# Block sums of v for the second batch by VectorE halving additions, second queries in two other banks, and placements issued ahead of loads

## The chip, the cores and the metric

The kernel runs on one core of one Trainium2 chip. The metric is the device time of one execution in microseconds (us). The engines are TensorE (PE; its weight loads are listed as PEld), VectorE (DVE), ScalarE (ACT), GpSimd (POOL) and the queue of SyncE (SP, listed as SPq), which issues every DMA of this kernel. Each works through its own list in order and waits on semaphores.

## The reference

Three stages follow each other: a sparse attention, a feed-forward layer with h * cos(h), and a second one with a normalised product. The change touches the attention and the first feed-forward steps behind it.

```
B, H, S, D = 2, 8, 768, 64;  block, window = 32, 16
k_sum = k.reshape(B, H, 24, 32, D).max(axis=3)
v_sum = v.reshape(B, H, 24, 32, D).mean(axis=3)
scores_l = q @ k.T / 8, kept where abs(i - j) < 16
scores_s = q @ k_sum.T / 8 + log(32)
a = softmax(concat(scores_l, scores_s))
out = a @ concat(v, v_sum)
x = out as [1536, 512]
h = x @ w_in;  x = (h * cos(h)) @ w_out
h = x @ w_in2; ln = normalised(h * softmax(h)) * g_ln;  out = ln @ w_out2
```

## The kernel before, in words

**Attention.** The 16 heads are worked in 8 pairs (n = 0 to 7; pairs 0 to 3 are the first batch, 4 to 7 the second), and each pair in 3 groups of four tiles of 64 queries, so there are 24 groups G. One loop, `for step in range(NGR + LA)`, runs 29 steps (0 to 28) as a software pipeline written by hand: step s issues the scores of group s+1 (`emit_s`, PE, tile `sps`), the masked maximum of group s (`emit_max`, DVE, then a subtraction by POOL), the exponential of s-1 (ACT), the sum and reciprocal of s-2 (DVE) with the normalising product (POOL), the transposes of s-4 (`emit_t`, PE, tile `aps`) with their copy out (`emit_at`), and the product with v of s-5 (`emit_av`, PE, tile `ops`) with its copy out (`emit_x`). Order within an engine is the order in which the code issues. The scores have two PSUM banks, used in turn, so the scores of G+2 can begin only when the maximum of G has read its bank.

**Keys and queries of a pair.** In the middle group of a pair (g == 1) `pair_k` and `pair_q` copy the loaded heads side by side (DVE for later pairs). In the last group (g == 2) PE transposes them (`emit_k`, `emit_q`) into the one tile `qk`; ACT then copies the queries out (`emit_qx`), DVE takes block maxima (`emit_ksum`), and ACT lays out the windows (`emit_kx`, `emit_kx_ends`). For pair 0 the queries go to two banks of their own, and DVE copies them out.

**v.** `load_v` fetches per pair 96-row windows with four DMAs into one of four buffers `vt`. Rows 96 to 119 of `vt` hold the 24 block means. `sum_v` makes the sums on PE with 12 matmuls against a strip of ones (tile `vsum`; the trace counts 24), `scale_v` scales them on ACT (`vm`), and `place_vsum` writes them with two DMAs. `VSUM_AT` gives the step of each pair; placement is issued at the end of the next step, behind that step's loads.

**Weights and fill.** The first feed-forward weights are turned into two parts beside the attention: ACT rewrites the raw words, DVE joins them (L171), ACT and POOL split them (L186, L187). `FILL` puts 3 or 4 of the first h products on PE per step from step 15. `drain` runs the cosine part of the first h tiles: u (ACT), n (DVE), sin (ACT), r (DVE), g (ACT and DVE). In the last steps DVE copies out the transposes (`DVE_AT` = 20) and the attention's result. Then the dense part begins with `emit_y(0)`.

## Time and profile before

| what | value |
|---|---|
| time, median of 3 runs | 496.52 us (492.27 to 496.61) |
| profiled execution: time, span | 493.17 us, 491.4 us |
| busy in the span: PE, DVE, ACT, POOL | 479.3, 303.0, 313.6, 152.6 us |
| 0 to 31.04 us (start, up to the scores of step 6): PE, DVE, ACT, POOL busy | 24.96, 17.46, 13.76, 13.11 us |
| 31.04 to 85.23 us (steps 6 to 21) | 53.96, 43.91, 45.67, 46.16 us of 54.19 |
| 85.23 to 103.49 us (steps 22 to 28) | 15.71, 15.70, 12.62, 10.33 us of 18.26 |
| 103.49 to 491.40 us (dense part) | 384.71, 225.98, 241.56, 82.97 us of 387.91 |

The span is what the trace covers; 1.77 us of the time lie around it. A row of the chain of waits has a start, a length and the work that the end hung on. A row of the timeline has a start, a length, the engine, the line and what it wrote from what; in brackets stands how long the engine stood idle before it and what ended that. "PEclk" is the granted TensorE clock as a share of 2.4 GHz.

### The profile page before, as it was taken

How to read it: one execution, taken by the hardware profiler on the slowest of the kernel's cores; microseconds unless marked ns; L12 is line 12 of the kernel's file. 1: busy time of each engine (PE TensorE's matmuls, PEld its weight loads, DVE VectorE, ACT ScalarE, POOL GpSimd, SP SyncE). 2: the span in 40 equal slices, each digit the busy share in tenths (PEclk: the TensorE clock that was granted, in tenths of full speed). 3: DMA queues.
4: the chain of work that ended last, by engine and by line, in shares of the span. 5: the costliest groups of instructions: out<-in, count | busy, mean ns of one | idle time of the engine just before them, and what ended most of it. 6: DMA issues, size and time to landing. Idle time of an engine off the chain costs nothing.

```text
span 491.4 us, 7884 instructions
## 1 busy us (share of the span) xinstructions
PE 479.3 (98%) x2943; PEld 394.5 (80%) x2943; DVE 303.0 (62%) x666; ACT 313.6 (64%) x539; POOL 152.6 (31%) x146
## 2 busy tenths in 40 slices
PE   8789999899999999999999999999999999999997
PEld 5668887678888888888888888888888888888886
DVE  3668976883445446556474655556477776776661
ACT  3669878756685766556655653788624867777621
POOL 3469977722432222222222220245500011110000
PEclk9889999999999999999999999999999999999999
DMA  8987854201222322332223220220001333223211
GB/s 258 285 199 210 212 135 127 87 2 43 87 85 90 122 88 87 92 122 88 87 91 120 88 86 27 94 96 0 0 2 43 87 90 83 65 64 65 69 40 43
DMA packets 59046, 46.17 MB, mean 94 GB/s; under 512 B 40448, under 2 KB 51328, under 8 KB 59008
## 3 DMA queue, kind: packets, MB, share of 16 engines
q1 hardware_dynamic: 59008, 45.67, 32.4%
q8 instruction: 23, 0.38, 0.3%
q14 instruction: 15, 0.12, 0.1%
HBM read 36.61 MB, written 3.15 MB: 81 GB/s over the span
## 4 chain that ended last, share of the span: by engine, by line
PE 88%; SPq 5%; POOL 2%; DVE 1%; ACT 1%; issue 1%; DMA 1%
PE y L276 27%; PE h L234 25%; PE o L865 13%; PE h L751 13%; PE sps L510 3%; SPq L393 3%; PE ops L565 2%; PE aps L547 2%; PE vsum L421 2%; SPq L357 1%; SPq L389 1%; POOL sm L525 1%; PE tp L799 1%; DMA vt<-vm 1%; POOL sm L540 1%
## 5 line engine op out<-in xcount | busy, mean ns | idle before, releaser
L234 PE MATMUL h<-xs,w 128*128 128x512 f32 x576 | 141.2, 391 | 0.0
L276 PE MATMUL y<-gs,w 128*128 128x512 f32 x576 | 138.1, 389 | 0.0
L276 PEld LDWEIGHTS y<-gs,w 128*128 128x128 f32 x576 | 108.1, 188 | 22.4
L234 PEld LDWEIGHTS h<-xs,w 128*128 128x128 f32 x576 | 107.2, 188 | 21.6
L187 POOL TENSOR_TENSOR w<-s,w 128x512 fp32r<-128x512 f32 x48 | 62.2, 1295 | 164.9 <-ACT w L186 141.9
L243 ACT ACTIVATE r<-h 128x512 int32<-128x512 f32 x48 | 28.7, 597 | 85.9 <-PE h L234 85.9
L248 DVE SCALAR_TENSOR_TENSOR r<-r,h 128x512 f32<-128x512 int32 x48 | 33.0, 687 | 67.4 <-ACT r L243 67.3
L865 PE MATMUL o<-w,ls 128*128 128x512 f32 (+1 forms) x312 | 67.8, 373 | 0.0
L751 PE MATMUL h<-w,xs 128*128 128x512 f32 x288 | 67.6, 390 | 0.0
L171 DVE SCALAR_TENSOR_TENSOR s<-raw 128x512 int32<-128x512 int32 x48 | 37.9, 790 | 44.8 <-ACT raw L164 38.3
L865 PEld LDWEIGHTS o<-w,ls 128*128 128x128 f32 x312 | 55.3, 188 | 10.7 <-DVE ls L841 0.4
L751 PEld LDWEIGHTS h<-w,xs 128*128 128x128 f32 x288 | 53.9, 188 | 11.1
L786 POOL TENSOR_TENSOR st<-st,mhalf 128x1 f32<-128x1 f32 x12 | 6.6, 550 | 110.1 <-DVE st L785 101.7
L204 POOL TENSOR_TENSOR xs<-X,xs 128x512 fp32r<-128x512 f32 x22 | 29.6, 1353 | 32.7 <-ACT xs L203 32.7
L253 ACT ACTIVATE r<-r,half_pi 128x512 f32<-128x512 f32 x48 | 34.5, 718 | 1.3 <-DVE r L248 1.3
L264 DVE TENSOR_TENSOR gs<-h,gs 128x512 fp32r<-128x512 f32 x48 | 32.6, 680 | 4.2 <-ACT gs L263 4.0
L258 DVE TENSOR_TENSOR h<-h,r 128x512 f32<-128x512 f32 x48 | 32.9, 686 | 0.4 <-ACT r L253 0.4
L163 ACT ACTIVATE raw<-raw 128x512 f32<-128x512 f32 x48 | 31.9, 664 | 0.0
L164 ACT ACTIVATE raw<-raw 128x512 int32<-128x512 uint32 x48 | 31.8, 663 | 0.0
L186 ACT ACTIVATE w<-s 128x512 fp32r<-128x512 f32 x48 | 30.1, 626 | 1.2 <-DVE s L171 0.9
L768 ACT ACTIVATE e<-h,st 128x1024 f32<-128x1024 f32 (+1 forms) x13 | 13.6, 1049 | 26.6 <-DVE st L764 23.1
L525 POOL TENSOR_TENSOR sm<-sm,mx 128x480 f32<-128x480 f32 x24 | 26.1, 1090 | 9.8 <-DVE mx L521 9.5
(81 smaller groups left out, 570.3 us busy)
## 6 DMA issues: line engine op xcount, KB each, us to landing
raw<-in_moe_w_in_dram SPq DMA_DIRECT2D x24, 512.0 KB, 3.6
raw<-in_moe_w_out_dram SPq DMA_DIRECT2D x24, 512.0 KB, 3.3
vt<-in_v_dram SPq DMA_DIRECT2D x16, 240.0 KB, 3.5
kt<-in_k_dram SPq DMA_DIRECT2D x8, 384.0 KB
qt<-in_q_dram SPq DMA_DIRECT2D x8, 384.0 KB, 7.7
out_dram<-osb SPq DMA_DIRECT2D x11, 256.0 KB, 2.0
vt<-vm SPq DMA_DIRECT2D x16, 72.0 KB
vt<-in_v_dram SPq DMA_DIRECT2D x16, 48.0 KB, 4.1
```

Source lines behind the costliest of these rows:

```text
L163: nc.scalar.activation(out=hw, in_=hw, func=AF.Prelu, scale=REBIAS, alpha=NEGATIVE)
L164: nc.scalar.activation(out=lw, in_=lw.bitcast(U32), func=AF.Copy, scale=TOP3)
L171: nc.vector.scalar_tensor_tensor(out=self.f32[i], in0=t[:, :, 1], scalar=3, in1=t[:, :, 0], op0=ALU.logical_shift_left, op1=ALU.bitwise_or)
L187: nc.gpsimd.tensor_tensor(out=w[:, 1, :], in0=f, in1=as32(w[:, 0, :]), op=ALU.subtract)
L234: nc.tensor.matmul(h, lhsT=w[:, a, f * P:(f + 1) * P], rhs=xs_of[tb, c][:, b_, :], start=(m == 0), stop=(m == 3 * KC - 1))
L248: nc.vector.scalar_tensor_tensor(out=r, in0=r.bitcast(I32), scalar=TWO_PI, in1=h_of[step], op0=ALU.mult, op1=ALU.subtract)
L253: nc.scalar.activation(out=r, in_=r, func=AF.Sin, scale=-1.0, bias=half_pi)
L258: nc.vector.tensor_tensor(out=h, in0=h, in1=r, op=ALU.mult)
L264: nc.vector.tensor_tensor(out=gs[:, 1, :], in0=r, in1=as32(gs[:, 0, :]), op=ALU.subtract)
L276: nc.tensor.matmul(y[e], lhsT=w[:, a, e * P:(e + 1) * P], rhs=gs[:, b_, :], start=(f == 0 and i == 0), stop=(f == GF - 1 and i == 2))
L751: nc.tensor.matmul(banks[n], lhsT=xs_of[NTB + t // TPB, c][:, a, t0:t0 + P], rhs=weights.done[w2i[c][n]][:, b_, :], start=(m == 0), stop=( ...
L865: nc.tensor.matmul(o, lhsT=ls_of[t][f // 4][:, a, s0:s0 + P], rhs=w[:, b_, cols], start=(f == 0 and i == 0), stop=(f == NF2 - 1 and i == 2))
```

## The change

It has five parts. (1) For the second batch, `load_blocks` loads v again for four heads at a time with each block of 32 rows on one of 96 partitions; `sum_blocks` adds halves on DVE (1024, 512, 256, 128 and 64 elements per partition), and `place_blocks` scales on ACT and writes with four DMAs. PE's sums for pairs 4 to 7 go. (2) The queries of pair 1 use the two banks of pair 0's, and DVE copies them out, after the keys' windows have been issued. (3) v of pair 0 is loaded before keys and queries of pair 2, its sums move from step 3 to step 1, and all placements move to the head of the next step, ahead of that step's loads. (4) The cosine steps of the first h tiles follow a table: u and n of tiles 0 and 1 come in steps 22 and 23. (5) All transposes are copied out by ACT, and that copy is issued before the drain.

```diff
@@ -94,7 +94,6 @@
     WSTEPS = (4, 7, 10, 13, 16, 19, 20, 21)
     XS = (7, 10, 13, 16)
     IDLE = (0, 0, 0)
-    DVE_AT = 20
     DVE_X = 19
     DVE_NORM = 99
     LAST = 5
@@ -321,15 +320,22 @@
 
         nc.scalar.activation(out=small[:, 1:2], in_=small[:, 0:1], func=func)
 
-    STAGES = ((emit_sin, 2), (emit_r, 2), (emit_u, 1), (emit_n, 1), (emit_g, 2))
+    DRAIN = {
+        -2: ((emit_u, 0), (emit_n, 0)),
+        -1: ((emit_u, 1), (emit_n, 1)),
+        1: ((emit_sin, 0), (emit_r, 0)),
+        2: ((emit_sin, 1), (emit_r, 1), (emit_g, 0), (emit_u, 2), (emit_n, 2)),
+        3: ((emit_sin, 2), (emit_r, 2), (emit_g, 1)),
+        4: ((emit_g, 2),),
+        5: ((emit_u, 3), (emit_n, 3), (emit_sin, 3), (emit_r, 3)),
+    }
 
     def drain(k):
 
         if k == 0:
             table(AF.Sin)
-        for stage, at in STAGES:
-            if 0 <= k - at < GF and (stage, k - at) != (emit_g, GF - 1):
-                stage(k - at)
+        for stage, step in DRAIN.get(k, ()):
+            stage(step)
 
 
     def attention():
@@ -413,9 +419,7 @@
 
             def sum_v(n):
 
-                o = (ps_h0 if n < 6 else ps_qk).tile(
-                    [P, 512] if n < 6 else [P, 2, 2, S // 2], F32, tag="h" if n < 6 else "qk", name="vsum")
-                o = (o if n < 6 else o[:, 0, 0])[:, 0:P]
+                o = ps_h0.tile([P, 512], F32, tag="h", name="vsum")[:, 0:P]
                 for t in range(HALF):
                     for c in range(2):
                         nc.tensor.matmul(
@@ -423,6 +427,35 @@
                             rhs=v_t[n][0:WIN, HALF * c + t].rearrange("p j d -> p (j d)"),
                             start=(t == 0), stop=(t == HALF - 1))
                 vs_t[n] = o
+
+            vb_t, vb_sum = {}, {}
+            HEADS = 4
+
+            def load_blocks(i):
+
+                b, h = divmod(HEADS * i + NPAIR, H)
+                t = vb_t[i] = io.tile([HEADS * NS, BLOCK, D], F32, tag="vb", name="vb", bufs=1)
+                nc.sync.dma_start(
+                    out=t.rearrange("p k d -> p (k d)"),
+                    in_=v[b, h:h + HEADS].rearrange("h (b k) d -> (h b) (k d)", k=BLOCK))
+
+            def sum_blocks(i, half):
+                if not half:
+                    vb_sum[i] = io.tile([HEADS * NS, D], F32, tag="vbs", name="vbs", bufs=1)
+                t = vb_t[i]
+                for m in ((16,), (8, 4, 2, 1))[half]:
+                    nc.vector.tensor_tensor(
+                        out=t[:, 0:m] if m > 1 else vb_sum[i].rearrange("p (k d) -> p k d", k=1),
+                        in0=t[:, 0:m], in1=t[:, m:2 * m], op=ALU.add)
+
+            def place_blocks(i):
+                m = io.tile([HEADS * NS, D], F32, tag="vbm", name="vbm", bufs=1)
+                nc.scalar.activation(out=m, in_=vb_sum.pop(i), func=AF.Copy, scale=1.0 / BLOCK)
+                for h in range(HEADS):
+                    n, j = divmod(HEADS * i + NPAIR + h, 2)
+                    nc.sync.dma_start(
+                        out=v_t[n][WIN:KW, :, j, :],
+                        in_=m[h * NS:(h + 1) * NS].unsqueeze(1).to_broadcast([NS, NT, D]))
 
             def scale_v(n):
                 m = io.tile([P, 2 * D], F32, tag="vm", name="vm")
@@ -475,7 +508,7 @@
                     out=kx[:, :, WIN:KW], in_=ks_t.pop(n).unsqueeze(1).to_broadcast([P, NT, NS]), func=AF.Copy)
 
             def emit_q(n):
-                if n == 0:
+                if n < 2:
                     qk_t["q", n] = bank(2, "q0"), bank(3, "q1")
                 t, (a, b) = q_t.pop(n), qk_t["q", n]
                 for c in range(NR):
@@ -487,7 +520,7 @@
                 qx = io.tile([P, S], F32, tag="qx", name="qx")
                 rows = qx.rearrange("p (i r) -> p i r", r=NR)
                 src = qk_t.pop(("q", n))
-                if n == 0:
+                if n < 2:
                     for r in range(2):
                         nc.vector.tensor_scalar_mul(
                             rows[:, :, r * NR // 2:(r + 1) * NR // 2],
@@ -549,10 +582,7 @@
 
             def emit_at(G):
                 at = sm_p.tile([KW, NG, P], F32, tag="at", name="at", bufs=2)
-                if G >= DVE_AT:
-                    nc.vector.tensor_copy(at, at_t[G])
-                else:
-                    nc.scalar.activation(out=at, in_=at_t[G], func=AF.Copy)
+                nc.scalar.activation(out=at, in_=at_t[G], func=AF.Copy)
                 at_t[G] = at
 
             def emit_av(G):
@@ -586,9 +616,9 @@
             nc.sync.dma_start(out=mask.rearrange("p t k -> p (t k)"), in_=c_mask)
             load_k(1)
             load_q(1)
+            load_v(0)
             load_k(2)
             load_q(2)
-            load_v(0)
             nc.gpsimd.memset(small, 0.0)
             nc.gpsimd.memset(strip, 0.0)
             warm_up(8)
@@ -607,7 +637,9 @@
 
 
             LX, LN, LT, LA = 1, 2, 4, 5
-            VSUM_AT = {3: 0, 4: 1, 7: 2, 9: 3, 12: 4, 13: 5, 16: 6, 19: 7}
+            VSUM_AT = {1: 0, 4: 1, 7: 2, 9: 3}
+            VB_LOAD = {9: 0, 15: 1}
+            VB_SUM = {12: (0, 0), 14: (0, 1), 17: (1, 0), 19: (1, 1)}
             VLOAD_AT = {1: 1, 4: 2, 6: 3, 8: 4, 10: 5, 13: 6, 16: 7}
             for step in range(NGR + LA):
                 n, g = divmod(step, GPP)
@@ -615,6 +647,8 @@
                 ahead = 1 if step == 1 else n + 1 if g == 0 and 0 < n < NPAIR - 1 else 0
 
                 warm_up(IDLE[g] if step < min(FILL) else 0)
+                if step - 1 in VSUM_AT:
+                    place_vsum(VSUM_AT[step - 1])
                 if step + 1 < NGR:
                     emit_s(step + 1)
                 if step == 0:
@@ -648,9 +682,9 @@
                     emit_max(step)
                 if step == 1:
                     emit_ksum(ahead)
-                drain(step - NGR)
                 if LT <= step < NGR + LT:
                     emit_at(step - LT)
+                drain(step - NGR)
                 weights.finish()
                 if summed:
                     emit_norm(step - LN)
@@ -660,7 +694,6 @@
                     emit_kx(ahead)
                 if step == 1:
                     emit_kx_ends(1)
-                if step == 0:
                     emit_qx(1)
                 if g == 2 and n + 2 < NPAIR:
                     emit_qx(n + 2)
@@ -680,8 +713,12 @@
                     load_q(n + 3)
                 if step in VLOAD_AT:
                     load_v(VLOAD_AT[step])
-                if step - 1 in VSUM_AT:
-                    place_vsum(VSUM_AT[step - 1])
+                if step in VB_LOAD:
+                    load_blocks(VB_LOAD[step])
+                if step in VB_SUM:
+                    sum_blocks(*VB_SUM[step])
+                    if VB_SUM[step][1]:
+                        place_blocks(VB_SUM[step][0])
                 if step in VSUM_AT:
                     scale_v(VSUM_AT[step])
 
@@ -889,8 +926,7 @@
 
         for c in range(KC):
             xs_of[1, c] = split_x(1, c, xs_b, nc.vector if c % 2 else nc.gpsimd)
-        for k in range(LAST, 7):
-            drain(k)
+        drain(LAST)
         emit_y(0)
         emit_y(1)
         for step in range(4, NSTEP):
```

**SP in the first steps.** Of before, from the loads of q of pair 3 on (`kt`, `qt`, `vt` are the loads of k, q, v; `vt<-vm` is a placement):

```order
L357 DMA qt<-in_q_dram 128x2x384
L389 DMA vt<-in_v_dram 96x10x64
L393 DMA vt<-in_v_dram 96x2x64
L389 DMA vt<-in_v_dram 96x10x64
L393 DMA vt<-in_v_dram 96x2x64
L139 DMA raw<-in_moe_w_in_dram 128x1024 x2
L357 DMA kt<-in_k_dram 128x6x128
L357 DMA qt<-in_q_dram 128x2x384
L389 DMA vt<-in_v_dram 96x10x64
L393 DMA vt<-in_v_dram 96x2x64
L389 DMA vt<-in_v_dram 96x10x64
L393 DMA vt<-in_v_dram 96x2x64
```

Right behind these stand the four placements of pairs 0 and 1. Of the change, from the same load on:

```order
L363 DMA qt<-in_q_dram 128x2x384
L395 DMA vt<-in_v_dram 96x10x64
L399 DMA vt<-in_v_dram 96x2x64
L395 DMA vt<-in_v_dram 96x10x64
L399 DMA vt<-in_v_dram 96x2x64
L469 DMA vt<-vm 12x12x128 x2
L138 DMA raw<-in_moe_w_in_dram 128x1024 x2
L363 DMA kt<-in_k_dram 128x6x128
```

The placement of pair 0 now stands in front of two weight loads and of the loads of pair 4's k and q and of pair 2's v.

**DVE at steps 14 and 15.** Of the change, from the end of the maximum of step 14 (`mx`) to the first instruction of the maximum of step 15 (`vb` is the tile of blocks, `vbs` the sums, `ss` the softmax sums):

```order
L554 ISA mx 128x1
L170 SCALAR_TENSOR_TENSOR s<-raw 128x512
L447 TENSOR_TENSOR vb<-vb 96x512
L447 TENSOR_TENSOR vb<-vb 96x256
L447 TENSOR_TENSOR vb<-vb 96x128
L447 TENSOR_TENSOR vbs<-vb 96x64
L567 TENSOR_REDUCE ss<-sm_98 128x4
L568 RECIPROCAL ss<-ss 128x4
L488 TENSOR_REDUCE ksum<-qk 128x24
L554 ISA sm_100,mx<-sps,mask 128x120
```

Before, the reduction of `ss` followed the joining of the weight (`s<-raw`) directly. The addition of 1024 stands two steps earlier, behind the maximum of step 12.

**ACT in the last steps.** Of the change, from the copy of step 24's transposes (`at`) on (`r<-h` is u, `r<-r,half_pi` the sine, `gs` g):

```order
L585 ACTIVATE at<-aps 120x512
L321 ACT_TABLE_LOAD
L321 ACTIVATE small<-small 128x1
L585 ACTIVATE at<-aps 120x512
L252 ACTIVATE r<-r,half_pi 128x512
L585 ACTIVATE at<-aps 120x512
L252 ACTIVATE r<-r,half_pi 128x512
L262 ACTIVATE gs<-h 128x512
L242 ACTIVATE r<-h 128x512
L585 ACTIVATE at<-aps 120x512
```

Before, ACT had no copy of transposes there, four u and three sines and g stood behind the table load, and DVE made the copies.

## Rows read from the trace of the kernel before

**Rows 1.** The chain that ended last, shares of the span by engine (page)

```profile
PE 88%; SPq 5%; POOL 2%; DVE 1%; ACT 1%; issue 1%; DMA 1%
```

**Rows 2.** The same chain in order of time: start us, us, what

```profile
26.10 1.00 SPq L436
27.15 2.90 DMA vt<-vm
...
39.58 0.66 PE qk L443 x6
...
57.59 0.97 PE sps L510 x16
...
61.49 0.71 ACT qx L496
...
64.05 1.04 PE sps L510 x16
...
66.98 1.31 PE vsum L421 x24
...
77.69 1.41 PE vsum L421 x24
```

**Rows 3.** Timeline of the first steps: start us, us, engine, line, out<-in

```profile
12.18 0.81 ACT L496 ACTIVATE qx<-qk 128x768 f32<-128x768 f32 x1 [1.76 <-PE qk L482]
13.03 0.96 DVE L455 TENSOR_REDUCE ksum<-qk 128x24 f32<-128x768 f32 x1 [1.40 <-ACT qx L496]
14.41 3.36 SPq L393 DMA_DIRECT2D vt<-in_v_dram  x1
15.66 1.04 PE L510 MATMUL sps<-kx,qx 64*64 64x120 f32 x16 [2.54 <-ACT kx L474]
...
22.13 1.04 PE L510 MATMUL sps<-kx,qx 64*64 64x120 f32 x16
...
25.14 1.04 PE L510 MATMUL sps<-kx,qx 64*64 64x120 f32 x16
...
30.19 0.92 PE L565 MATMUL ops<-at,vt 120*64 120x64 f32 x16 [2.12 <-DMA vt<-vm]
...
34.48 1.04 PE L510 MATMUL sps<-kx,qx 64*64 64x120 f32 x16
```

**Rows 4.** Windows of PE: length, busy (instructions), granted clock, DMA share, GB/s

```profile
17.00:18.00 1.00, 1.00 (x6) 0.50 0.56 123
...
19.00:20.00 1.00, 1.00 (x10) 0.50 0.81 225
31.00:32.00 1.00, 1.00 (x12) 0.50 1.11 231
```

**Rows 5.** DVE additions by line: ns minimum/median/maximum, first and last start, forms

```profile
L204 DVE TENSOR_TENSOR xs<-X,xs x2: 1321/1550/1778, 105.3 to 106.5; 128x512 fp32r<-128x512 f32 x2
L841 DVE TENSOR_TENSOR ls<-s,ls x18: 677/684/1800, 382.2 to 467.2; 128x512 fp32r<-128x512 f32 x18
L771 DVE TENSOR_TENSOR e<-h,e x13: 692/1224/1225, 356.2 to 473.3; 128x1024 f32<-128x1024 f32 x11, 128x512 f32<-128x512 f32 x2
L787 DVE TENSOR_TENSOR st<-st x12: 159/160/161, 360.5 to 477.5; 128x1 f32<-128x1 f32 x12
```

**Rows 6.** Timeline: the two POOL instructions beside DVE's two of line 204

```profile
104.72 3.00 POOL L204 TENSOR_TENSOR xs<-X,xs 128x512 fp32r<-128x512 f32 x2 [8.74 <-ACT xs L203]
```

**Rows 7.** Windows: length, busy of PE, PEld, DVE, ACT, POOL, clock, DMA

```profile
50.63:64.05 13.42, 13.30 (x209) 11.19 (x208) 12.12 (x47) 11.41 (x25) 12.49 (x11) 1.00 0.77 186
64.05:68.29 4.24, 4.24 (x65) 3.50 (x67) 4.21 (x13) 3.67 (x8) 4.17 (x5) 1.00 0.37 129
68.29:85.23 16.94, 16.82 (x231) 13.61 (x230) 10.59 (x54) 13.46 (x28) 12.87 (x13) 1.00 0.58 144
```

**Rows 8.** Waits of PE from 84 to 104 us: total us, times, longest

```profile
PE aps L547 <- DVE at L553: 1.6, 2, 0.9
PE aps L547 <- ACT at L555: 0.8, 2, 0.5
```

## What I predict

> **What bounds the kernel now.** The chain of waits comes first: PE holds 88% of it [rows 1], and from 103.49 us on PE is busy 384.71 of 387.91 us, in work that the change leaves alone. So the change can act only on the moment at which the dense part begins. The chain in order of time then says what that moment hangs on: in the first 30 us on SP and a placement of v [rows 2], later on PE with the sums of v on it (1.31 and 1.41 us) [rows 2]. The timeline of the start shows three PE waits or slow stretches that belong together: scores of step 2 wait 2.54 us, behind block maxima that themselves waited 1.40 us for ACT's copy of the queries [rows 3]; the first product with v waits 2.12 us for its placement [rows 3]; and after each of the two idle stretches the granted clock is 0.50, so 1.2 instead of 2.4 GHz, for about 3 us [rows 4]. Last, the windows of the middle show who could become the bound when PE sheds work: in 50.63 to 64.05 us DVE is busy 12.12 of 13.42 us and POOL 12.49 [rows 7]. DVE and POOL are nearly as full as PE there.
>
> **The start: queries of pair 1, v first, placements ahead.** The block maxima no longer stand behind ACT's copy, so they start at 13.03 - 1.40 = 11.63 us. From their start to the scores it took 15.66 - 13.03 = 2.63 us [rows 3], so these could start at 14.26. The sums of pair 0, 1.31 us [rows 2], now fill PE's idle time, which began at 15.66 - 2.54 = 13.12, and end at 14.43; I take that, 1.2 us earlier than before. DVE's two query copies replace its 1.40 us of idle time. Then come scores (0.97), transposes of keys (0.66) and of queries (the same again) [rows 2]: 16.72. From the start of a query copy to the scores that wait for it it takes 64.05 - 61.49 = 2.56 us [rows 2], so the scores of step 4 start at 19.28 instead of 22.13 [rows 3]. From there to the next scores 25.14 - 22.13 = 3.01 us [rows 3], so 22.29; and from those to the scores two steps on 64.05 - 57.59 = 6.46 us, in a stretch with the same work and no wait for a placement [rows 2]: 28.75 instead of 34.48 [rows 3]. That is 5.7 us. The placement of pair 0 is not what comes late next: its sums end at 14.43, SP is free at 14.41 + 3.36 = 17.77 [rows 3], and four placements took from 26.10 to 30.05 [rows 2], so two land before 21.8. PE asks for them 30.19 - 2.12 - 25.14 = 2.93 us after the scores at 22.29 [rows 3], at 25.2; 3.4 us are the cover. What does come late is PE itself: with the sums moved away from step 3 it idles from 16.72 + 0.97 = 17.69 to 19.28, 1.6 us. Idle stretches of 2.54 and 2.12 us were each followed by the half clock [rows 3, 4]; three us at 0.50 lose 1.5. So the gain is 5.7 without and 4.2 with such a stretch. The nearest row, 2.12 us, speaks for it; I take **-4.5 us**. Keys and queries of pair 2 now load behind 576 KB of v; DVE, their first user, has the two query copies to do before them, and that is the cover. If it is too short, each us that they land late is lost at the scores of step 4.
>
> **The first load of blocks, steps 12 to 15.** PE sheds two sums, 2.6 us. DVE gets five additions. An addition of 1024 takes 1.224 us, of 512 0.684, of one element 0.160 [rows 5]; on the line between the last two, 256, 128 and 64 take 0.42, 0.29 and 0.23. Each waits for the one before it, so they add up: 1.22 + 0.68 + 0.42 + 0.29 + 0.23 = 2.84 us. They also meet POOL. DVE's additions with both inputs in SBUF took 0.684 alone and 1.321 and 1.778 beside POOL [rows 5], while POOL's two took 3.00 us [rows 6]: a wait of 0.64 and 1.09 us each. POOL is busy 93% of the stretch [rows 7], so each of five additions can wait between 0 and 1.09; half of that, 0.5, is 2.5 us. DVE's demand is then 12.12 + 2.84 + 2.5 = 17.46 us in a stretch of 13.42, or **+4.0 us**. The ends are 12.12 + 2.84 - 13.42 = +1.5 (no wait at all) and, with five times 1.09, +7.0. Nothing of PE's 2.6 us comes through, since the next scores wait for DVE's maximum, and that stands behind the additions. ACT's scaling of the sums waits for the last addition at the head of ACT's queue, with the split of a weight, an exponential and a copy of transposes behind it; POOL and PE wait for these. This is inside the +7.0. The extra load of 768 KB meets DMA shares of 0.77, 0.37 and 0.58 [rows 7], and its placements are wanted three steps later, in step 17: nothing.
>
> The Trainium skill (SBUF — State Buffer, Who interferes with whom) says that a VectorE instruction with two SBUF inputs and a GpSimd instruction that reads SBUF shut each other out, the later one waiting until the other is finished. It speaks against this change, since by it a short addition waits as long as a long one. A reader of the rows alone might take a factor, 1.55 / 0.684 = 2.27, and get 2.84 x 2.27 = 6.4 us of additions and +5.1 us for this stretch instead of +4.0.
>
> **The second load, steps 16 to 21.** PE sheds 1.31 + 1.41 = 2.7 us [rows 2]. DVE is busy 4.21 + 10.59 of 21.18 us [rows 7], so 6.4 us are idle and the additions, 2.84 + 2.5 = 5.3, have room on the whole. But one addition stands ahead of the block maxima and four ahead of a maximum for which scores wait, so I take **0**, with -2.7 (all hidden) and 5.3 - 2.7 = +2.6 (nothing hidden) as ends.
>
> **The last steps.** PE waited 1.6 us for DVE's copies of transposes and 0.8 for ACT's [rows 8]. ACT now issues these copies ahead of the cosine work, and four of the first tiles' instructions move into steps 22 and 23. I take **-1.6 us**; the ends are -2.4 and 0, the latter if the n of tiles 0 and 1, which now stand ahead of the last weights on DVE, hand their delay on through POOL.
>
> **Sum.** -4.5 + 4.0 + 0 - 1.6 = -2.1 us, and 493.17 - 2.1 = 491.1, so 491 us. The profiled execution was 3.35 us below the median of the runs shown and 0.9 above the lowest. About 1%, 4.9 us, is what a measurement of this kernel can tell from no change.
>
> **Rivals.** (a) *The additions are hidden.* POOL waits for DVE's results, so it may run dry whenever DVE is late, and the additions meet nobody. For it: POOL's next operands come from DVE's maximum and reciprocal. Against it: POOL busy 93%. Then +1.5 in the first stretch and -2.7 in the second: -4.5 + 1.5 - 2.7 - 1.6 = -7.3, so 485.9 us. (b) *The start does not move.* The change then doesn't do what it says: v of pair 0, or the keys and queries behind it, land too late, and only the 1.2 us of the first scores come: -1.2 + 4.0 - 1.6 = +1.2, so 494.4 us. For it: the DMA queue had SP held for 3.36 us at one load [rows 3]. Against it: the same bytes in another order. (c) *Slower: DVE's additions take the place of PE as the bound in both stretches.* Each addition waits a full POOL instruction, 1.09 us, which decides from about 0.9 on; PE then idles over 4 us at step 15 and gets the half clock once more, 1.5 us: -4.2 + 7.0 + 2.6 + 1.5 = +6.9, so 500.1 us. For it: the two rows beside POOL [rows 5]. Against it: POOL has few instructions ready while DVE stands still.
>
> **How the numbers follow.** Forecast 0.46, with 488 to 494 as its own range; (a) 0.32, 483.5 to 488; (b) 0.12; (c) 0.10. Faster by over 1% means below 488.2: 0.9 of (a) and about an eighth of the forecast, 0.34. Slower by over 1% means above 498.1: most of (c), 0.08. The rest is 0.58. The range from 485 to 497.5 leaves out a third of (a) and most of (c), under 2 in 10.
>
> **What will show it.** Start: the scores of step 2 near 14.4 us, no wait of the first product with v for a placement, the scores of step 7 between 28.8 and 30.3; the clock at 0.50 or not near 21 us tells the two ends apart. First load: additions of 1024 longer than 1.3 us and of 64 near 0.23 plus a wait, and PE waiting for DVE's maximum at step 16; additions at their bare prices speak for (a). Last steps: no PE wait for copies of transposes. I am wrong if PE stays full through steps 12 to 16, or if the start to step 7 moves by less than 3 us.

## The result: 0.5% slower, and what the profile after shows

The kernel after took 496.07 us, the median of 20 runs (493.71 to 498.32); the kernel before, beside it, 493.62 of 20 (490.99 to 496.61). The ratio is 1.0052, with a 95% interval of 1.0034 to 1.0069, so 1.7 to 3.4 us slower. I had forecast 2.1 us faster. The profiled execution of after took 494.23 us with a span of 492.4, against 493.17 and 491.4 before: 1.06 us. It lies 1.84 us below its median, that of before 0.45 below its own, which is the rest of the difference.

Chain of waits of after, shares by engine, the line that answers to [rows 1]:

```profile
PE 83%; DVE 8%; ACT 3%; DMA 2%; SPq 2%; issue 1%; POOL 0%; DVEq 0%; ACTq 0%
```

DVE holds 8% where it held 1%. **The start** moved by nearly what I had said. Timeline of PE's first steps in after, as in [rows 3] (start us, us, engine, line, out<-in, idle time before):

```profile
14.95 1.04 PE L543 MATMUL sps<-kx,qx 64*64 64x120 f32 x16
...
17.86 1.04 PE L543 MATMUL sps<-kx,qx 64*64 64x120 f32 x16 [0.42 <-DVE mx L554]
20.29 1.04 PE L543 MATMUL sps<-kx,qx 64*64 64x120 f32 x16 [1.39 <-DVE mx L554]
...
26.17 0.69 PE L595 MATMUL ops<-at,vt 120*64 120x64 f32 x16
...
29.84 1.04 PE L543 MATMUL sps<-kx,qx 64*64 64x120 f32 x16 [0.82 <-DVE mx L554]
```

Scores of step 2 start at 14.95 instead of 15.66, the first product with v waits for no placement, and scores of step 7 start at 29.84 instead of 34.48: 4.64 us. What came late were keys and queries of pair 2; DVE's copies of them stand ahead of the maxima for which the scores of steps 3 and 4 wait:

```profile
14.27 0.56 DVE L381 COPY kg<-kt 128x768 f32<-128x768 f32 x1 [0.95 <-DMA kt<-in_k_dram]
...
15.59 0.56 DVE L381 COPY qg<-qt 128x768 f32<-128x768 f32 x1 [0.77 <-DMA qt<-in_q_dram]
```

**The first load of blocks** then takes a part back. Timeline of DVE, POOL and ACT around its additions (DVE L447):

```profile
48.82 1.45 DVE L447 TENSOR_TENSOR vb<-vb 96x1024 f32<-96x1024 f32 x1
49.16 1.97 POOL L558 TENSOR_TENSOR sm<-sm,mx 128x480 f32<-128x480 f32 x1
...
55.79 1.44 POOL L558 TENSOR_TENSOR sm<-sm,mx 128x480 f32<-128x480 f32 x1
56.30 2.92 DVE L447 TENSOR_TENSOR vb<-vb 96x512 f32<-96x512 f32 x3
57.19 1.43 POOL L573 TENSOR_TENSOR sm<-sm,ss 128x480 f32<-128x480 f32 x1
59.26 0.22 DVE L447 TENSOR_TENSOR vbs<-vb 96x64 f32<-96x64 f32 x1
59.52 0.26 ACT L453 ACTIVATE vbm<-vbs 96x64 f32<-96x64 f32 x1 [2.48 <-DVE vbs L447]
```

Five additions take 1.45 + 2.92 + 0.22 = 4.59 us where their bare prices sum to 2.84. For the second load it is 2.00 + 3.20 + 0.22 = 5.42:

```profile
70.16 2.00 DVE L447 TENSOR_TENSOR vb<-vb 96x1024 f32<-96x1024 f32 x1
...
76.15 3.20 DVE L447 TENSOR_TENSOR vb<-vb 96x512 f32<-96x512 f32 x3
```

The chain of waits in order of time runs through them into the scores of step 16:

```profile
56.38 1.40 DVE vb L447
...
57.81 1.11 DVE vb L447
...
59.26 0.22 DVE vbs L447
...
60.18 0.94 DVE ksum L488
...
61.98 1.06 PE sps L543 x7
```

Windows of the four stretches from step 12 on, with the columns of [rows 7]; the cuts are the starts of the scores of steps 12, 16, 17 and 22 and of the first dense product:

```profile
45.91:61.98 16.07, 10.88 (x163) 8.84 (x159) 14.98 (x52) 11.89 (x25) 13.98 (x11) 1.00 1.00 260
61.98:66.37 4.39, 4.39 (x39) 3.56 (x39) 4.36 (x13) 2.21 (x5) 3.98 (x4) 0.62 0.65 121
66.37:84.58 18.21, 15.70 (x211) 12.38 (x207) 16.12 (x58) 13.11 (x28) 13.03 (x12) 1.00 0.55 140
84.58:104.41 19.83, 15.80 (x181) 11.74 (x181) 13.77 (x39) 15.39 (x30) 11.02 (x12) 1.00 0.34 105
```

In the first, PE is busy 10.88 of 16.07 us, and a stretch at clock 0.62 follows. Last, the waits of PE from 84 to 105 us, which answer to [rows 8]:

```profile
PE aps L580 <- ACT at L585: 3.2, 4, 1.4
PE ops L595 <- DVE X L607: 0.9, 2, 0.5
```

The waits for copies of transposes were to vanish; they are 3.2 us instead of 2.4, all of them now for ACT. The 0.9 us for copies of the result (`X`) are new.

The chain of waits runs into this stretch from the additions of step 19: behind the last of them stand ACT's scaling, an exponential and the rewriting of a raw weight, behind these DVE's joining of that weight, and so on to the last weights:

```profile
79.39 0.23 DVE vbs L447
...
79.80 0.59 ACT sm L563
80.39 0.55 ACT raw L162
...
81.53 1.39 DVE s L170
```

The four terms, by the starts of PE's scores: start -4.64 (forecast -4.5), steps 12 to 16 16.07 - 13.49 = +2.58 (+4.0), steps 16 to 22 22.60 - 21.18 = +1.42 (0), from there to the first dense product 19.83 - 18.26 = +1.57 (-1.6). The sum is +0.93. The dense part begins at 104.41 instead of 103.49 and is as long as before (387.99 and 387.91 us).

### The profile page after: what moved, and what is told of

Its sections match the earlier page's. It is cut to its first block, busy times and chain, and to the rows that moved or that the text cites. A ratio compares the mean times of both kernels' runs of the same rounds, so it can differ in the third digit from the quotient of the medians.

```text
span 492.4 us, 7695 instructions
## 1 busy us (share of the span) xinstructions
PE 472.2 (96%) x2847; PEld 387.6 (79%) x2847; DVE 309.8 (63%) x674; ACT 314.5 (64%) x540; POOL 154.6 (31%) x146
## 4 chain that ended last, share of the span: by engine, by line
PE 83%; DVE 8%; ACT 3%; DMA 2%; SPq 2%; issue 1%; POOL 0%; DVEq 0%; ACTq 0%
PE y L275 27%; PE h L233 25%; PE o L902 13%; PE h L788 13%; DMA qt<-in_q_dram 2%; DVE vb L447 2%; DVE sm L554 2%; PE sps L543 1%; SPq L399 1%; DVE s L170 1%; DVE ksum L488 1%; DVE ss L567 1%; PE aps L580 1%; PE ops L595 1%; PE tp L836 1%
## 5 line engine op out<-in xcount | busy, mean ns | idle before, releaser
L543 PE MATMUL sps<-kx,qx 64*64 64x120 f32 x384 | 25.5, 274 | 10.6 <-DVE mx L554 9.0
L558 POOL TENSOR_TENSOR sm<-sm,mx 128x480 f32<-128x480 f32 x24 | 28.0, 1167 | 11.2 <-DVE mx L554 11.0
```

## Experiments

All lengths below are worked out from the starts of PE's scores, as above. "12-16" is step 12 to step 16, "last" step 22 to the first dense product. A row is one profiled execution of its kernel; ratios and medians are of several. "last" repeats well: the five kernels with PE's sums and the old last steps (before, e1, e5, e9, e12) lie between 18.24 and 18.27 us. "12-16" does not: it holds waits for loads that differ from one execution to the next.

```
kernel                     step 7  step 12  12-16  16-22   last  dense from
before                      34.48    50.56  13.49  21.18  18.26  103.49
after                       29.84    45.91  16.07  22.60  19.83  104.41
e1 start                    29.55    45.62  14.13  21.17  18.24   99.16
e2 start, sums              30.66    46.99  17.17  22.65  19.38  106.19
e3 start, last steps        30.87    46.95  16.11  21.18  18.74  102.98
e4 sums                     36.15    52.22  16.08  22.84  19.37  110.51
e5 start, fillers           30.60    47.49  20.35  21.19  18.25  107.28
e6 start, sums by reduction 31.04    47.51  16.57  23.21  18.25  105.54
e7 after, no additions      32.70    48.78  12.91  18.63  19.30   99.62
e8 after, scale later       29.97    46.04  17.84  23.42  19.87  107.17
e9 start, sum 5 later       30.30    46.53  13.30  22.41  18.27  100.51
e10 start, copies           29.98    46.06  15.36  21.18  18.37  100.97
e11 start, order            31.43    48.50  14.40  21.16  19.09  103.15
e12 start, sum 5, fillers   30.51    47.02  13.31  22.77  18.25  101.35
e13 after, POOL left out    29.90    46.27  14.94  23.75  18.75  103.71
e14 after, blocks earlier   30.74    46.82  16.69  22.44  19.84  105.79
```

My theory was that the four terms are separate and add up. Rival 1: the start's gain is given back by a full middle. Rival 2: the last steps only inherit lateness from the additions.

**e1: the start alone.**

```
-            VSUM_AT = {1: 0, 4: 1, 7: 2, 9: 3}        # after
+            VSUM_AT = {1: 0, 4: 1, 7: 2, 9: 3, 12: 4, 13: 5, 16: 6, 19: 7}
```

Blocks, additions and the new last steps go; sums of v are all PE's again.

> The kernel before with the start alone (v of pair 0 ahead of the keys and queries of pair 2, sums of pair 0 in step 1, placements ahead of loads, queries of pair 1 in banks 2 and 3); sums of v all by PE, last steps as before. Theory (the terms add up, the start keeps its gain): -4.6 us against before, the 4.64 us by which step 7 starts earlier in the changed kernel, so a ratio near 0.991, and y near 98.9 us in the trace. Rival 1 (the gain of the start is given back, because DVE, busy 12.12 of 13.42 us in steps 12 to 15, and POOL bound the middle whatever PE does): not over 1.5 us faster, y at 102 us or later.

Ratio 0.9961 (0.9929 to 0.9993), a median of 492.49 us. In the trace, that of the fastest of its 12 executions (488.86 us), the dense part begins 4.33 us earlier: there the gain is kept to the end, and rival 1 falls. But the medians show 1.25 us of it, within what rival 1 allowed for the time; of 12 executions five stayed at a mean clock of 1.000 (mean 490.2 us) and seven fell to 0.997 or 0.993 (492.4 to 495.6). Before, none of 29 reached 1.000.

**e2: start and sums, the last steps as before.**

```
+                if G >= DVE_AT:                        # 20
+                    nc.vector.tensor_copy(at, at_t[G])
...
+        for stage, at in STAGES:
+            if 0 <= k - at < GF and (stage, k - at) != (emit_g, GF - 1):
+                stage(k - at)
```

> The changed kernel with the last steps as before (old order of the cosine work, copies of transposes from step 20 on by DVE): start and sums by VectorE stay. Theory (last steps cost +1.6 us of their own, sums +2.6 +1.4): -4.6 + 4.0 = -0.6 us against before, so about 2 us faster than the changed kernel; in the trace step 22 starts near 84.6 us as there, but the first product of the dense part near 102.9 instead of 104.4. Rival 2 (the waits of the last steps are only lateness handed on from the additions): same time as the changed kernel, +1 to +2.5 us against before.

Ratio 1.002 (0.9992 to 1.0049), so not shown to be faster than after (1.0034 to 1.0069). Steps 12 to 16 are 1.1 us longer than in after; DVE waited 0.64 us for the first load of blocks and 0.62 for the second. The last stretch fell only from 19.83 to 19.38 us, not to 18.26. So 0.45 us of the +1.57 was the last steps' own; the other 1.1 came with the sums. Both theories were half right.

**e3: start and last steps, sums by PE.** As e1, but from the last steps of after nothing is undone:

```
-            VSUM_AT = {1: 0, 4: 1, 7: 2, 9: 3}        # after
-            VB_LOAD = {9: 0, 15: 1}
-            VB_SUM = {12: (0, 0), 14: (0, 1), 17: (1, 0), 19: (1, 1)}
+            VSUM_AT = {1: 0, 4: 1, 7: 2, 9: 3, 12: 4, 13: 5, 16: 6, 19: 7}
```

> The changed kernel with all sums of v by PE, no load of blocks and no additions: start and last steps stay. Theory: -4.6 + 1.6 = -3.0 us against before, so 1.6 us slower than the start alone; PE still waits over 2 us for ACT's copies of transposes in steps 23 to 26. Rival 2 (last steps carry nothing of their own, sums carry all): -4.6 us or, with the -1.6 us that I had forecast for the last steps, -6.2 us, and PE waits under 1 us for these copies.

Ratio 0.9974 (0.9944 to 1.0003), 0.22 us in the medians from e1, where I had expected 1.6. Last stretch 18.74 us, 0.5 more than e1, by the same measure as e2. Steps 12 to 16 are long for another reason, which the waits of PE from 42 us on show:

```profile
PE vsum L427 <- DMA vt<-in_v_dram: 2.3, 1, 2.3
PE aps L553 <- ACT at L558: 2.1, 3, 1.3
PE ops L568 <- DVE X L580: 0.9, 2, 0.5
```

The sums of pair 5, in step 13, waited 2.3 us for v that is loaded from step 10 on.

**e4: the sums alone**, in the kernel before.

> The kernel before with the block sums of the second batch by VectorE alone (loads of blocks at steps 9 and 15, additions at steps 12, 14, 17, 19); start and last steps as before. Theory: +2.6 in steps 12 to 16 and +1.4 in steps 16 to 22, so +4.0 us against before (ratio 1.008). Rival 3 (the additions cost only because PE arrives 4.6 us earlier at a DVE that is full; with PE as late as before they are hidden): within 1.5 us of before.

Ratio 1.010 (1.006 to 1.014), +5.3 us. In the trace +2.6, +1.7 and +1.1 in the three stretches, nearly the same as in after for the first two and as in e2 for the last; the second holds a wait of 1.43 us of DVE for a load of blocks. The sums by DVE cost this much whether PE comes early or late: rival 3 falls. The trace was also 1.7 us late at step 7 already, in a part that this edit does not touch.

**e5: start and fillers.**

```
-                warm_up(IDLE[g] if step < min(FILL) else 0)
+                warm_up({3: 6}.get(step, 0))
```

> The start alone, with six of the start's filler products (128x512, result unused) put ahead of the scores of step 4, where PE idled 1.82 us in the run of the start alone. Theory (PE's idle stretches at the start decide in which executions the clock falls to half, and that is why a start that brings 4.3 us in the trace brings 1.3 to 1.9 us in the medians): fewer executions below a mean clock of 1.000 than 7 of 12, a median near 490.2 us, the mean of those that stayed at 1.000, a ratio near 0.992. Rival 4 (the half clock comes from places elsewhere in the program): the same share of executions below 1.000, median near 492.5, and the fillers may cost up to 0.5 us.

Ratio 0.996 (0.9927 to 0.9992), eight of 12 below 1.000: no better than e1, as rival 4 said. The profiled execution was the slowest of the 12 (496.93 us), so it shows one way to lose time and not how often. In it the idle stretch ahead of step 4 was 0.53 us instead of 1.82 and the start kept its clock, but the sums of pair 5 waited 4.0 us for v, and the clock was 0.50 from 56 to 62 us. Timeline of PE:

```profile
57.21 2.92 PE L421 MATMUL vsum<-vt,strip 96*64 96x128 f32 x24 [4.00 <-DMA vt<-in_v_dram]
60.05 1.87 PE L510 MATMUL sps<-kx,qx 64*64 64x120 f32 x16
```

**e6: reductions instead of additions.**

```
-                for m in ((16,), (8, 4, 2, 1))[half]:
-                    nc.vector.tensor_tensor(
-                        out=t[:, 0:m] if m > 1 else vb_sum[i].rearrange("p (k d) -> p k d", k=1),
-                        in0=t[:, 0:m], in1=t[:, m:2 * m], op=ALU.add)
+                d = slice(half * D // 2, (half + 1) * D // 2)
+                nc.vector.tensor_reduce(
+                    out=vb_sum[i][:, d], in_=t[:, :, d].rearrange("p k d -> p d k"), op=ALU.add, axis=AX.X)
```

> Start and block sums by VectorE with the last steps as before, the five additions of a load replaced by two reductions of 1024 elements (half of the columns each, all 32 rows at once; same loads, same steps, same result). A reduction has one input in SBUF; the row sums of 484 elements took 642 to 653 ns in all 24 cases, whatever POOL did. Theory (the additions cost because POOL and they wait for each other): by the step from 0.64 us for 484 to 0.94 for 768 elements a reduction takes about 1.2 us, never over 1.3; steps 12 to 16 near 13.4 + 1.0 = 14.5 us (start with additions: 17.2), last steps under 18.8, first dense product near 100.5 us (106.2). Rival 5 (any 2.4 to 2.8 us more on a DVE that is full cost the same): steps 12 to 16 at 15.5 us or more, first dense product at 103 us or later.

Ratio 0.9983 (0.9956 to 1.0011) against 1.002 of e2; the intervals overlap, so that reductions are faster is not shown in the time. The reduction's line in the trace (ns minimum/median/maximum):

```profile
L441 DVE TENSOR_REDUCE vbs<-vb x4: 1928/1936/1942, 51.8 to 78.9; 96x32 f32<-96x1024 f32 x4
...
  DMA vb<-in_v_dram: 3.6, 2
```

They never vary with POOL, as expected, but take 1.94 us, not 1.2: I had priced them by row sums of neighbouring elements, and these read elements 64 apart (whether the distance is what costs, no run separates). The last stretch is back at 18.25 us. By its numbers rival 5 came true: steps 12 to 16 took 16.57 us and the first dense product came at 105.54. But DVE also waited 3.6 us for the two loads of blocks (1.30 and 2.27), so e6 doesn't decide between theory and rival.

**e7: four of five additions left out.**

```
-                for m in ((16,), (8, 4, 2, 1))[half]:
+                for m in ((), (1,))[half]:
```

> The changed kernel without four of each load's five additions: only the last, of 64 elements, is done, so the block sums are of two rows instead of 32. Loads, scaling and placements stay. Theory (the additions are the cost): steps 12 to 16 at 13.5 us or less (16.07), 16 to 22 at 21.2 or less (22.60), last steps near 18.8 (19.87), first dense product near 99.5 us (104.4). Rival 6 (the loads of 768 KB are: queries of the next pair landed 7 us after their issue behind one, and DVE waited 0.63 us): steps 12 to 16 stay over 15 us.

From step 12 to the dense part 50.84 us instead of 58.50, one trace of each. The four additions of each load cost **7.7 us**. With loads, scaling and placements still there, steps 12 to 22 took 31.54 us, against 34.67 before, and rival 6 falls. PE's 2.7 us then come through in steps 16 to 22 (18.63 instead of 21.18). The last stretch stays at 19.30, though: my 18.8 missed. The two additions of 64 elements that were left took 1002 and 617 ns, where those behind another addition took 220 to 222. Each met a POOL instruction that had begun, and ended within 0.1 us of its end:

```profile
57.67 1.44 POOL L558 TENSOR_TENSOR sm<-sm,mx 128x480 f32<-128x480 f32 x1
...
58.19 1.00 DVE L447 TENSOR_TENSOR vbs<-vb 96x64 f32<-96x64 f32 x1
...
72.81 0.99 POOL L573 TENSOR_TENSOR sm<-sm,ss 128x480 f32<-128x480 f32 x1
...
73.27 0.62 DVE L447 TENSOR_TENSOR vbs<-vb 96x64 f32<-96x64 f32 x1
```

**e8: scaling one step later.**

```
+                if step - 1 in VB_SUM and VB_SUM[step - 1][1]:
+                    place_blocks(VB_SUM[step - 1][0])
...
-                    if VB_SUM[step][1]:
-                        place_blocks(VB_SUM[step][0])
```

> The changed kernel with the scaling of the block sums on ACT and its placements one step later (steps 15 and 20 instead of 14 and 19). In the changed kernel ACT waited 2.48 and 1.95 us at the head of its queue for the last addition. Theory (this wait is part of the price: a weight's split, an exponential and copies of transposes stand behind it): the last steps fall from 19.87 to about 18.8 us, steps 12 to 16 from 16.07 by up to 1 us. Rival 7 (what counts is DVE's maximum behind the additions, ACT's wait lies beside it): both stretches within 0.3 us of the changed kernel.

Neither stretch got shorter (17.84 and 19.87 us). For the last steps rival 7 holds: to move ACT's scaling away gained nothing. Steps 12 to 16 are outside both, 1.8 us longer; the first load's additions took 5.87 us there instead of 4.59, and DVE waited 0.53 us for the load.

**e9: pair 5's sums in step 14**, on e1.

```
-            VSUM_AT = {1: 0, 4: 1, 7: 2, 9: 3, 12: 4, 13: 5, 16: 6, 19: 7}
+            VSUM_AT = {1: 0, 4: 1, 7: 2, 9: 3, 12: 4, 14: 5, 16: 6, 19: 7}
```

> The start alone, with PE's sums of pair 5 in step 14 instead of 13 (they read v that is loaded at step 10; pair 5's products come in step 20). In two of four runs with all sums by PE and the new start the traces show PE waiting for that load, 2.3 and 4.0 us. Theory (what the medians of the start alone lack against its trace comes from this load landing late in some executions, and from the half clock behind it): no wait of the sums for v in the trace, median 491.0 us or less, ratio near 0.993. Rival 8 (it comes from PE's idle stretch ahead of step 4): median as for the start alone, ratio 0.996.

Ratio 0.9939 (0.9914 to 0.9964), median 491.05; 12-16 is 13.30 us, and no execution fell below a mean clock of 0.996 or took over 492.24 us (e1: up to 495.62). That fits the theory that the late load is what the start alone lost, but doesn't show it: the interval overlaps that of e1 (0.9929 to 0.9993), and in its trace steps 16 to 22 took 22.41 us instead of 21.17, more than 12-16 gained.

**e10 and e11: the halves of the last steps**, each on e1. e10 has the copies on ACT ahead of the cosine work:

```
-                if G >= DVE_AT:
-                    nc.vector.tensor_copy(at, at_t[G])
-                else:
-                    nc.scalar.activation(out=at, in_=at_t[G], func=AF.Copy)
+                nc.scalar.activation(out=at, in_=at_t[G], func=AF.Copy)
...
-                drain(step - NGR)
                 if LT <= step < NGR + LT:
                     emit_at(step - LT)
+                drain(step - NGR)
```

e11 has the new order of the cosine work:

```
-        for stage, at in STAGES:
-            if 0 <= k - at < GF and (stage, k - at) != (emit_g, GF - 1):
-                stage(k - at)
+        for stage, step in DRAIN.get(k, ()):
+            stage(step)
...
-        for k in range(LAST, 7):
-            drain(k)
+        drain(LAST)
```

> The start alone and of the last steps one half: copies of transposes from step 20 on by ACT, ahead of the cosine work, whose order stays as before. Last steps (scores of step 22 to the first dense product) with neither half 18.24 us, with both 18.74. Theory (the new order of the cosine work is what costs: u of tiles 0 and 1 stand on ACT, n on DVE ahead of the last weights): 18.24 - 0.8 = 17.4 us, PE waits for copies under 1 us. Rival 9 (the copies on ACT wait behind the splits of weights and the exponentials, where DVE had room): 18.7 us or more, PE waits for copies over 2 us.

> The start alone and of the last steps the other half: the new order of the cosine work, copies of transposes from step 20 on by DVE and behind it, as before. Theory: 18.7 us or more, and PE waits for DVE's copies, now behind n of tiles 0 and 1, over 2.4 us. Rival 9: 18.24 us or less.

18.37 and 19.09 us against 18.24, one execution of each. The order alone costs 0.85 us, as the theory said; the copies on ACT alone bring nothing (+0.13, not -0.8). The halves don't add up: both together cost 0.50 (e3), so behind the new order ACT's copies win back 0.35. Waits of PE in e11 for copies of transposes:

```profile
PE aps L554 <- ACT at L562: 2.3, 2, 1.3
PE aps L554 <- DVE at L560: 1.2, 2, 0.6
```

It is ACT's copies that come late, more than DVE's as I wrote there: in ACT's queue u of tiles 0 and 1 stands ahead of them. In after the copy stands ahead of u in its own step, but u and n still hold up the last weight. DVE's n of tile 0 (89.76 us) waits for u and stands ahead of the joining (90.37), and ACT waits for that to split the weight:

```profile
91.08 0.63 ACT L185 ACTIVATE w<-s 128x512 fp32r<-128x512 f32 x1 [1.08 <-DVE s L170]
```

By the chain of waits POOL's part of the weight (91.79), its next subtraction (93.02) and ACT's copy of transposes (94.55), for which PE waits, stand behind this split.

**e12: start, pair 5's sums in step 14 and fillers.**

> The start alone with both: sums of pair 5 in step 14, and six filler products ahead of the scores of step 4. If both the late load and the idle stretch ahead of step 4 bring the half clock, each in some executions: most of 12 executions at a mean clock of 0.997 or above, median near 490.3 us, ratio 0.992 to 0.993, faster than each alone. If the lower clock comes from elsewhere: no better than the start alone, 0.996.

Ratio **0.9915 (0.9885 to 0.9946)**, median 490.69 of 7 runs, all at 0.999 or 1.000: faster than before, 3.6 us below the median beside it (494.30), and the lowest ratio here. Faster than each of the two alone is not shown: e9's median, taken beside the same runs of before, is 0.36 us away. Its steps 16 to 22 still hold a wait of 1.29 us of the sums of pair 6 for v.

**e13: POOL's work around the additions left out.**

```
+                if 12 <= G <= 20:      # emit_max, ahead of POOL's subtraction
+                    return
...
+                if 10 <= G <= 18:      # emit_norm
+                    return
```

> The changed kernel with POOL's two operations of a step left out around the additions: no subtraction of the maxima for steps 12 to 20 and no scaling by the row sums for groups 10 to 18 (so the weights of these groups are not normalized). POOL keeps only the low parts of weights and inputs there; DVE's additions stay as they are. Theory (the additions are long because each waits for a POOL instruction): 1024, 512, 256, 128 and 64 elements fall to 1.22, 0.68, 0.42, 0.29 and 0.23 us, 2.84 us a load instead of 4.59 and 5.42, but for one or two that meet a low part. Rival 10 (a chain of additions in place on one tile is slow by itself, or slowed by the transfers): 512, 256 and 128 elements stay at 1.28, 1.09 and 0.62 us on the mean.

DVE's additions by shape in e13 (busy us, mean ns, idle before):

```profile
L447 DVE TENSOR_TENSOR vb<-vb 96x1024 f32<-96x1024 f32 x2 | 2.4, 1222 | 3.1 <-DMA vb<-in_v_dram 3.1
L447 DVE TENSOR_TENSOR vb<-vb 96x512 f32<-96x512 f32 x2 | 1.4, 682 | 0.0
L447 DVE TENSOR_TENSOR vb<-vb 96x256 f32<-96x256 f32 x2 | 0.8, 420 | 0.1
L447 DVE TENSOR_TENSOR vb<-vb 96x128 f32<-96x128 f32 x2 | 0.6, 290 | 0.1
L447 DVE TENSOR_TENSOR vbs<-vb 96x64 f32<-96x64 f32 x2 | 0.4, 222 | 0.1
```

The same five in after:

```profile
L447 DVE TENSOR_TENSOR vb<-vb 96x1024 f32<-96x1024 f32 x2 | 3.5, 1726 | 0.0
L447 DVE TENSOR_TENSOR vb<-vb 96x512 f32<-96x512 f32 x2 | 2.6, 1276 | 0.0
L447 DVE TENSOR_TENSOR vb<-vb 96x256 f32<-96x256 f32 x2 | 2.2, 1095 | 0.1
L447 DVE TENSOR_TENSOR vb<-vb 96x128 f32<-96x128 f32 x2 | 1.2, 623 | 0.1
L447 DVE TENSOR_TENSOR vbs<-vb 96x64 f32<-96x64 f32 x2 | 0.4, 221 | 0.1
```

Without these POOL instructions beside them they are at the bare prices of the prediction, within 0.01 us; rival 10 falls. The dense part begins only 0.7 us earlier; here, too, DVE waited for the blocks, 0.65 and 2.43 us. So how much of the 7.7 us of e7 is the waiting for POOL and how much the additions themselves, no run shows. The last stretch is 18.75 us, as in e3 without any blocks (18.74): what the additions add there is gone.

**e14: blocks with more room.**

```
-            VB_LOAD = {9: 0, 15: 1}
-            VB_SUM = {12: (0, 0), 14: (0, 1), 17: (1, 0), 19: (1, 1)}
+            VB_LOAD = {7: 0, 15: 1}
+            VB_SUM = {12: (0, 0), 14: (0, 1), 18: (1, 0), 19: (1, 1)}
```

> The changed kernel with the first load of blocks two steps earlier (step 7 instead of 9) and the second load's first addition one step later (18 instead of 17). In five of the six other kernels with these loads DVE stood 0.5 to 2.4 us at the first addition for one of them, though not in the profiled execution of the changed kernel. Theory (the loads land late in most executions, which is why the medians show +2.5 us and that one trace +1.0): no wait of DVE for a block in the trace, median about 1.4 us below the changed kernel's 496.07, ratio to before near 1.002. Rival 11 (the additions alone make the loss, the wait for a load lies beside other waits): ratio 1.005 as before.

No wait for a block in the trace, and yet a ratio of 1.0071 (1.0043 to 1.0099), no better than after. That speaks against the late load as what the medians hold beyond the trace, and for rival 11. It is one trace, and the addition of 1024 now stands one step before the other four of its load, so the edit changes two things.

## Why the prediction was wrong, step by step

- **The start, -4.5, was right in size in the traces** (-4.64 in after, -4.33 to the end in e1), in part by luck, since another sum than mine gives it. I had it as 5.7 less 1.2 to 1.5 for a half clock near 21 us. In after the clock stayed at 1.00 there; what came late was the other thing I named, keys and queries of pair 2: the scores of step 4 start at 20.29, not 19.28, after DVE had waited 0.95 and 0.77 us for them.
- **The first load, +4.0, was too dear** (+2.58). The mechanism is shown: additions wait for POOL (e13), 4.59 - 2.84 = 1.75 us for this load, not 2.5. The second load's waited 5.42 - 2.84 = 2.58. The sum also took DVE's other work as fixed at 12.12 us; it was 14.98 - 4.59 = 10.39, mostly because its copies of keys and queries took 1.30 us instead of 2.41 and its two joinings 2.03 instead of 2.48. DVE also stood idle for 1.09 us. The Trainium skill (SBUF — State Buffer, Who interferes with whom) says that of a VectorE instruction with two SBUF inputs and a GpSimd instruction that reads SBUF the one that comes second is blocked until the first is done, and that a reduction on trn2 never contends. This case's traces agree: 64 elements took 617 and 1002 ns when they met POOL first (e7), and the reductions 1928 to 1942 throughout (e6).
- **The second load, 0, failed.** I let DVE's 6.4 idle us in the stretch cover the additions. The stretch grew by 1.42 us, where without four of the five additions PE's shed work gave -2.55 (e7 against before). So the idle time did not cover them; that it lies between waits, not at the steps where the additions stand, is how I read it.
- **The last steps, -1.6, are the step that turned the sign**: +1.57. Two things stood against it. The new last steps cost 0.50 us by themselves (e3), the order alone 0.85 (e11). I had put no cost on the order. The path that after shows I had named for my end of 0, that the n of tiles 0 and 1 hand their delay on through POOL: from u and n over the joining, ACT's split and POOL to a copy that PE waits for. That end was not low enough. And the additions of step 19 reach into this stretch: about 1.1 us in e2 and e4, none with reductions (e6) or without POOL's work beside them (e13). I had ended the additions' account at step 22. They reach there by ACT, which comes late: its copy of transposes about the scores of step 22 starts 0.51 us after these scores in after and e2, and 0.58 or 0.57 before them in e3 and e13. The 19.30 us of e7 fit this: PE was earlier there, and the copy started with the scores. The 19.87 of e8 do not, with the copy 0.02 us before them, so that first copy is not all of it; the rest stays open.
- **The loads of blocks at nothing** holds in after and e7. In e2, e4, e6, e8 and e13 DVE waited 1.3 to 3.6 us in all for them, so the cover that I saw is thin; e14, with no such wait, was no faster.
- The rivals: (a), additions hidden, falls with 4.59 and 5.42 us for 2.84; (b) fell with step 7 at 29.84; (c), slower because DVE becomes the bound in both stretches, has the mechanism, at under half its price (+4.0 us in both stretches, not +9.6); its sum leaves out the last steps, for which (a) and (b) have -1.6.

Why the medians show 2.45 us and the traces 1.06 is settled only as far as that the profiled execution of after had the second lowest time of its 20; where the others lost more, no trace shows. The terms above are those of single executions. In the medians the start alone brought 1.25 us (e1), start and sums together lost 1.58 (e2), and after lost 2.45. Measured so, the start is the term that missed by most, 3.25 us of its -4.5, though each of these medians has an interval of about 1 us or more to either side. Whether after loses its start's gain as e1 does is open: the sums of pair 5, which e9 moved, are not on PE there.

## What to carry to other kernels

Work that moves from the bounding engine to a nearly full one must be costed where the instructions stand, and up to the point where that engine has caught up again, not only to the end of the stretch. Here DVE additions with both inputs in SBUF took up to nearly twice their price beside POOL (5.42 us for 2.84); the reductions kept theirs, but over elements 64 apart that was high (1.94 us for 1024). Ask of each product what it waits for long before its result is wanted: the start alone had a ratio of 0.9961, with one sum a step later 0.9939, and with six fillers besides 0.9915, though the intervals overlap. And a term that one trace confirms may not be in the medians: -4.33 us in the trace of e1 were -1.25 there.

## What the runs showed that I had not expected

The same idle stretch is followed by the half clock in one execution and not in another. PE idled 1.82 us ahead of step 4 in e1 and in e7. Windows of e1 and then of e7 (length, busy of PE, PEld, DVE, ACT, POOL, clock, DMA):

```profile
22.00:24.00 2.00, 2.00 (x37) 1.67 (x33) 2.00 (x3) 1.46 (x5) 2.00 (x2) 1.00 1.01 359
```

```profile
22.00:24.00 2.00, 2.00 (x22) 2.00 (x20) 2.00 (x3) 0.57 (x2) 2.00 (x2) 0.50 0.98 373
```

In e7 scores of step 6 start 3.2 us later for it (29.65 against 26.49). Executions of one kernel lie in groups by mean clock: in e1 490.2 us on the mean at 1.000, 493.5 at 0.997, 493.7 at 0.993. The one trace of e1 is of the best of them. That less idle time ahead of step 4 makes the half clock rarer is not shown: e5, with 0.53 us of it in its trace, had eight of 12 executions below 1.000, e1 seven.
